# Sparse attention and a four-expert MoE on one core: strided-head loads position by position, a second layer block by block, other numbers in the planner

## The chip, the cores and the metric

One core of a Trainium2 chip runs the whole program. The metric is the device time of one launch in microseconds. One kernel's runs beside another's show differences down to about 1%.

## The reference

Batch 4, 8 heads, 576 positions, 64 values a head, all in float32. Heads 0 to 3 are local (a position sees the 32 positions up to itself), heads 4 to 7 strided (it sees the earlier positions that are equal to it modulo 32). The result, 2304 tokens of 512, goes through four dense experts, all of them for every token.

```
scores = scale * np.matmul(q, k.transpose(0, 1, 3, 2))
mask_local = (rel >= 0) & (rel < stride)                       # stride 32
mask_strided = (rel >= 0) & (pos[None, :] % stride == pos[:, None] % stride)
scores = np.where(masks[None, :, :, :], scores, -1000000000.0)
scores = scores - np.max(scores, axis=-1, keepdims=True)
attn = np.exp(scores); attn = attn / (np.sum(attn, axis=-1, keepdims=True) + 1e-09)
x = np.matmul(attn, v).transpose(0, 2, 1, 3).reshape(B * S, H * D)
for e in range(E):
    h = np.maximum(x @ w1[e], 0.0)
    out += p[:, e:e + 1] * (h @ w2[e])
```

## The kernel before

**Attention.** Two heads make a pair; the 16 pairs run in the order of channels 0, 2, 1, 3 of each batch, so that local (L) and strided (S) pairs alternate. A pair loads q, k, v (`load_qk`, L312 and L318; `load_v`, L328, L332, L339), TensorE transposes q and k (L380, L385), ScalarE evicts them (L344), TensorE makes the scores (L420), VectorE adds the mask and takes the maximum (L429, L434), VectorE or GpSimd subtracts it (L437), ScalarE does the exponential (L442), VectorE the sums (L446 to L448), VectorE or GpSimd the division (L451), TensorE transposes the weights (L477) and multiplies by v (L507), ScalarE evicts into the token buffers (L543, L553), and VectorE subtracts there for the low part (L546). A pair is done in two groups.

**Strided pairs.** Position 32 i + r with residue r sees only positions of its residue: 32 small problems of 18 positions. A partition holds 12 residues of one position, 3 x 18 = 54 partitions a head, partition 18 u + i with u = 0 to 2 and residue r = 10 u + j. All loads are issued by SyncE, one queue, on which at most eight are outstanding: each waits for the one eight before it. The q, k and v tiles of strided pairs are single.

**MoE.** A unit is one expert and one half of its hidden size, eight in all. `plan_first` takes all eight for the first 512 tokens (96 matmuls of 512 columns a unit: L630 the first layer, L646 the second), between the attention's work and after it. Then two parts of 896 tokens take each unit by a product scheme of seven products (L767). Every operand is split in a high and a low part, and three products are made of them: high x high, high x low, low x high. The second layer adds 12 matmuls a bank: `PASS` goes through the three kinds and, within each, the four hidden blocks f. hs 0 to 3 (ScalarE, L634) are the high parts of the blocks, hs 4 to 7 (VectorE, L637) the low parts; `order` shows them as hs_120 to 123 and hs_124 to 127.

**Order.** The program is laid out once by `Plan.run`: each operation has an engine, a duration in us, its tokens and a priority; a list scheduler places the operations and each engine gets its instructions in order of planned start. On the chip each engine runs its list in that order and waits at its head. While TensorE is planned idle before the first MoE matmul, matmuls on zeros are put in (`idle`, L891).

Of the kernel before, what the change touches and what calls it, by code (L numbers as in the profile page):

```python
# [20 lines left out]
VZ = 4.0  # L21
# [3 lines left out]
class Op:  # L25
    __slots__ = ("eng", "dur", "fn", "nxt", "wait", "ready", "prio", "bank", "start", "end", "moe", "cols", "idx")


class Plan:


    SYNC = 0.12
    TICK = 4096 / 1200
# [10 lines left out]
    def add(self, eng, dur, fn, reads=(), writes=(), prio=0.0, bank=None, moe=False, cols=0):  # L44
# [6 lines left out]
        o.cols = cols  # L51
        o.ready = 0.0
# [21 lines left out]
    def run(self, idle):  # L74
# [6 lines left out]
        credit = 0.0  # L81
# [62 lines left out]
        while left:  # L144
# [64 lines left out]
def attn_moe_kernel(  # L209
# [94 lines left out]
    def load_qk(n, which, g):  # L304
# [3 lines left out]
        if kd == "L":  # L308
            t = t[kd][buf(n)]
# [12 lines left out]
    def load_v(n, g):  # L322
        b, c = order[n]
        a = v[b, 2 * c]
        if c < 2:
            t = vst["L"][buf(n)]
            if g != 1:
                nc.sync.dma_start(  # L328
                    out=t[32:LW, 0, :, :], in_=bass.AP(a.tensor, a.offset, [[D, 64], [S * D, 2], [1, D]]))
            t0, t1 = ((1, 4), (4, LT))[g] if g is not None else (1, LT)  # L330
# [15 lines left out]
    def plan_pair(n):  # L346
# [10 lines left out]
        if kd == "L":  # L357
            for g in (0, 1) if n < 4 else (None,):
                gs = (0, 1) if g is None else (g,)
                z = zg[gs[0]]  # L360
                for which, nm in enumerate(("qst", "kst")):
                    add("SP", 1.65 if g is None else 0.95, lambda which=which, g=g: load_qk(n, which, g), (),
                        [f"{nm}L{bf}{i}" for i in gs], z - 16)
                add("SP", 2.4 if g is None else 1.42, lambda g=g: load_v(n, g), (), [f"vstL{bf}{i}" for i in gs], z - (VZ if n < 4 else 0))
        else:
            add("SP", 1.3, lambda: load_qk(n, 0, None), (), ["qstS00", "qstS01"], zg[0] - 16)
            add("SP", 1.3, lambda: load_qk(n, 1, None), (), ["kstS00", "kstS01"], zg[0] - 16)
            add("SP", 2.6, lambda: load_v(n, None), (), ["vstS00", "vstS01"], zg[0] - (VZ if n < 4 else 0))


        for g in range(2):
            z = zg[g]
            for nm, t, dst in (("q", qstv, qTv), ("k", kstv, kTv)):
                key = ("ps", n, "a", nm, g)

                def tr(key=key, t=t, g=g):
# [563 lines left out]
```

## Time and profile before

| | us |
|---|---|
| median of 3 runs (903.64, 907.44, 909.93) | 907.44 |
| the profiled execution | 903.7 |
| its span, first to last instruction | 901.9 |
| TensorE busy | 872.9 (97%) |
| VectorE, ScalarE, GpSimd busy | 528.1, 346.7, 227.8 |
| chain that ended last: TensorE, DMA, VectorE | 87%, 6%, 3% |

A row of the timeline has its start and length, the engine, the line and the tiles (buffer numbers left out: ps and mo are PSUM banks). A busy TensorE need not be at full rate: the granted clock says at which of its two levels (1.2 or 2.4 GHz, 0.5 or 1.0) it ran.

### The profile page before, as it was taken

What the parts mean: (1) busy time and instruction counts of PE and PEld (TensorE: products, weight loads), DVE (VectorE), ACT (ScalarE), POOL (GpSimd) and SP (SyncE); (2) the same over time, 40 slices, a digit from 0 to 9 for tenths busy, and PEclk for the clock granted to TensorE, in tenths of its full rate; (3) what the DMA queues carried; (4) which work ended last, traced back from release to release, by engine and by line L of the source; (5) the groups of instructions that cost most, each with busy time, mean ns of one, the idle gap of its engine ahead of it and who ended that gap; (6) DMA issues with size and microseconds to landing.
All of it is one profiled execution on the core that took longest, in us unless ns stands there. A gap on an engine that the chain in (4) does not pass through costs nothing.

```text
span 901.9 us, 13147 instructions
## 1 busy us (share of the span) xinstructions
PE 872.9 (97%) x5240; PEld 743.1 (82%) x5240; DVE 528.1 (59%) x790; ACT 346.7 (38%) x685; POOL 227.8 (25%) x187
## 2 busy tenths in 40 slices
PE   6889899998999999999999999999999999999998
PEld 4667677786888898888988988889889888898897
DVE  2574676759546455745646656586466574564553
ACT  2563454545223242432523524435235243252340
POOL 1241110326224121321312314152133132131200
PEclk8798899998999999999999999999999999999999
DMA  4474544311222201211211112111111121121002
GB/s 104 129 203 137 142 139 143 93 63 50 92 94 99 99 36 47 93 47 48 88 38 63 47 47 94 47 60 63 36 65 48 47 94 47 47 85 43 15 1 81
DMA packets 65117, 67.95 MB, mean 75 GB/s; under 512 B 36512, under 2 KB 38624, under 8 KB 65056
## 3 DMA queue, kind: packets, MB, share of 16 engines
q1 hardware_dynamic: 65056, 67.12, 23.7%
q8 instruction: 41, 0.67, 0.3%
q14 instruction: 20, 0.16, 0.1%
HBM read 62.39 MB, written 4.72 MB: 74 GB/s over the span
## 4 chain that ended last, share of the span: by engine, by line
PE 87%; DMA 6%; DVE 3%; SPq 2%; ACT 1%; issue 1%; POOL 0%; ACTq 0%; POOLq 0%; DVEq 0%
PE mo L646 26%; PE ps L646 17%; PE ps L767 15%; PE mo L767 15%; PE mo L630 7%; DMA kstS<-in_k 2%; PE ps L420 2%; PE ps L477 1%; PE ps L507 1%; DMA vstS<-in_v 1%; DMA vstL<-in_v 1%; DMA raw<-in_moe_w 1%; PE ps L385 1%; PE ps L380 1%; SPq L318 1%
## 5 line engine op out<-in xcount | busy, mean ns | idle before, releaser
L574 ACT ACTIVATE w2h<-raw 128x512 fp32r<-128x512 f32 x88 | 51.1, 622 | 264.1 <-PE mo L646 144.1
L646 PE MATMUL mo<-w2h,h 128*128 128x512 f32 (+1 forms) x456 | 121.2, 387 | 0.0
L646 PE MATMUL ps<-w2h,h 128*128 128x512 f32 (+1 forms) x448 | 119.0, 387 | 0.0
L655 DVE SCALAR_TENSOR_TENSOR acc<-mo,pr,acc 128x512 f32<-128x512 f32 (+1 forms) x77 | 57.4, 745 | 101.6 <-PE mo L646 101.4
L646 PEld LDWEIGHTS mo<-w2h,h 128*128 128x128 f32 x456 | 85.2, 188 | 17.1
L646 PEld LDWEIGHTS ps<-w2h,h 128*128 128x128 f32 x448 | 83.8, 188 | 16.9
L575 POOL TENSOR_TENSOR w2l<-raw,w2h 128x512 fp32r<-128x512 f32 x27 | 37.9, 1406 | 210.9 <-ACT w2h L574 210.8
L637 DVE SCALAR_TENSOR_TENSOR h<-c,h 128x448 fp32r<-128x448 f32 x96 | 83.7, 884 | 8.8 <-ACT h L634 5.3
L655 DVE SCALAR_TENSOR_TENSOR acc<-ps,pr,acc 128x512 f32<-128x512 f32 (+1 forms) x50 | 37.2, 744 | 66.1 <-PE ps L646 65.8
L646 PE MATMUL mo<-w2h,hs 128*128 128x512 f32 x256 | 72.7, 415 | 3.3 <-ACT hs L634 3.2
L575 DVE TENSOR_TENSOR w2l<-raw,w2h 128x512 fp32r<-128x512 f32 x61 | 59.0, 979 | 15.8 <-ACT w2h L574 15.8
L634 ACT ACTIVATE h<-c 128x448 fp32r<-128x448 f32 x96 | 54.5, 576 | 27.1 <-DVE c L796 25.5
L646 PEld LDWEIGHTS mo<-w2h,hs 128*128 128x128 f32 x256 | 50.0, 199 | 16.6 <-ACT hs L634 5.7
L646 PE MATMUL mo<-w2l,h 128*128 128x512 f32 (+1 forms) x228 | 60.6, 387 | 0.0
L646 PE MATMUL ps<-w2l,h 128*128 128x512 f32 (+1 forms) x224 | 59.5, 387 | 0.0
L646 PEld LDWEIGHTS mo<-w2l,h 128*128 128x128 f32 x228 | 42.6, 188 | 8.9
L646 PEld LDWEIGHTS ps<-w2l,h 128*128 128x128 f32 x224 | 41.9, 188 | 8.7
L783 ACT ACTIVATE u<-mo 128x448 f32<-128x448 f32 x48 | 26.1, 545 | 46.0 <-PE mo L767 45.7
L796 DVE TENSOR_TENSOR c<-mo,u 128x448 f32<-128x448 f32 x48 | 29.5, 615 | 19.8 <-PE mo L767 19.2
L796 DVE TENSOR_TENSOR c<-ps,u 128x448 f32<-128x448 f32 x48 | 29.5, 615 | 19.7 <-PE ps L767 19.7
L646 PE MATMUL mo<-w2l,hs 128*128 128x512 f32 x128 | 39.4, 421 | 0.0
L783 ACT ACTIVATE u<-ps 128x448 f32<-128x448 f32 x48 | 26.1, 545 | 29.0 <-PE ps L767 28.7
(239 smaller groups left out, 1739.9 us busy)
## 6 DMA issues: line engine op xcount, KB each, us to landing
raw<-in_moe_w SPq DMA_DIRECT2D x44, 1024.0 KB
out<-acc SPq DMA_DIRECT2D x17, 256.0 KB
qstS<-in_q SPq DMA_DIRECT2D x16, 162.0 KB
kstS<-in_k SPq DMA_DIRECT2D x16, 162.0 KB
vstS<-in_v SPq DMA_DIRECT2D x32, 81.0 KB
vstL<-in_v SPq DMA_DIRECT2D x12, 192.0 KB
qstL<-in_q SPq DMA_DIRECT2D x12, 144.0 KB
kstL<-in_k SPq DMA_DIRECT2D x12, 144.0 KB
```

Source lines behind the costliest of these rows:

```text
L318: nc.sync.dma_start(out=t[:, h].rearrange("p t d -> p (t d)"), in_=bass.AP(a.tensor, a.offset + h * S * D, [[10 * D, 3], [32 * D, 18], [1, ...
L420: nc.tensor.matmul(s[a, o:o + W], lhsT, rhs, start=True, stop=True)
L574: add("ACT", 0.62, lambda: nc.scalar.activation(out=hi(), in_=src(), func=AF.Copy), [tok], [name + "h"], z)
L575: add("VP", VP, lambda e: engine(e).tensor_tensor(out=lo(), in0=src(), in1=hi().bitcast(F32), op=ALU.subtract), [tok, name + "h"], [name + ...
L630: nc.tensor.matmul(pt[:, 0:TA], w[:, c % 2, (f % 2) * P:(f % 2) * P + P], (xl if i == 1 else xh)[c], start=j == 0, stop=j == 11)
L634: nc.scalar.activation(out=dst(), in_=src(), func=AF.Relu)
L637: nc.vector.scalar_tensor_tensor(out=dst(), in0=src(), scalar=0.0, in1=hi().bitcast(F32), op0=ALU.max, op1=ALU.subtract)
L646: nc.tensor.matmul(pt, ht[f][:, ts], wt[f][:, cs], start=j == 0, stop=j == 11)
L655: nc.vector.scalar_tensor_tensor(out=a, in0=pt, scalar=sc, in1=a, op0=ALU.mult, op1=ALU.add)
L767: nc.tensor.matmul(pt, wq[a][i == 2][:, j, f * P:f * P + P], xq[b][i == 1][j], start=bool(first) and n == 0, stop=True, skip_group_check=True)
L783: add("ACT", 0.55, lambda: nc.scalar.activation(out=late["u"][i], in_=held[key][:, 0:TH], func=AF.Copy), [key, "late2"], [f"u{i}"], zz)
L796: add("DVE", 0.6, lambda: nc.vector.tensor_tensor(out=late["c"][c], in0=held[key][:, 0:TH], in1=late["u"][i], op=ALU.add), [key, f"u{i}"], ...
```

## The change

1. `load_qk` and `load_v` for strided pairs: the source's outer dimension is 18 (positions), then 3, then the contiguous residues. Partition 3 i + u takes the place of 18 u + i; the mask, and the source and target patterns of the evictions (`xsrc`, `cols`), follow.
2. The first four pairs' local loads are no longer issued in two parts (`g` goes away).
3. The second layer's 12 matmuls go hidden block by hidden block, three kinds for each.
4. The planner: other durations (only two lines shown), 0.18 us after a TensorE operation before another engine may use it, and loads that follow each other on one modelled wire.

```diff
+    DRAIN = 0.18
+    LAND = 1.9
             if e == "SP":
-                o.end += 2.1
+                wire = max(wire, o.end) + o.xfer
+                o.end = wire + self.LAND
...
-                x.ready = max(x.ready, o.end + (self.SYNC if x.eng != e else 0.0))
+                x.ready = max(x.ready, o.end + (self.SYNC + self.DRAIN * (e == "PE") if x.eng != e else 0.0))
...
-            ts = slice(0, 6) if g is None else slice(3 * g, 3 * g + 3)
             for h in range(2):
                 nc.sync.dma_start(
-                    out=t[:, ts, h, :], in_=src[b, 2 * c + h].rearrange("(t p) d -> p t d", p=LW)[:, ts])
+                    out=t[kd][buf(n)][:, :, h, :], in_=src[b, 2 * c + h].rearrange("(t p) d -> p t d", p=LW))
...
                     out=t[:, h].rearrange("p t d -> p (t d)"),
-                    in_=bass.AP(a.tensor, a.offset + h * S * D, [[10 * D, 3], [32 * D, 18], [1, 12 * D]]))
+                    in_=bass.AP(a.tensor, a.offset + h * S * D, [[32 * D, 18], [10 * D, 3], [1, 12 * D]]))
...
-                        in_=bass.AP(a.tensor, a.offset + (h * S + 6 * par) * D, [[10 * D, 3], [32 * D, 18], [1, 6 * D]]))
+                        in_=bass.AP(a.tensor, a.offset + (h * S + 6 * par) * D, [[32 * D, 18], [10 * D, 3], [1, 6 * D]]))
...
-                add("ACT", (0.3, 0.33)[c > 1], ev, [key], [f"{nm}T{kd}{bf}{g}"], z + 0.2)
+                add("ACT", (0.41, 0.44)[c > 1], ev, [key], [f"{nm}T{kd}{bf}{g}"], z + 0.2)
...
-            dd = nel / 960 + 0.07
+            dd = nel / 960 + 0.15
...
-                        return bass.AP(a.tensor, a.offset, [list(a.ap[0]), [1, 6], [10, 3], [32, i1 - i0]])
+                        return bass.AP(a.tensor, a.offset, [list(a.ap[0]), [1, 6], [32, i1 - i0], [10, 3]])
...
-        passes = list(enumerate(PASS))
+        passes = list(enumerate((i, f) for f in range(NKF) for i in range(3)))
...
-    strided = (p // 18 == c // 18) & (c % 18 <= p % 18) | (p >= 54)
+    strided = (p % 3 == c % 3) & (c // 3 <= p // 3) | (p >= 54)
```

SyncE, the first loads after those of pair 0's first half and the masks. Before (qstL_131 is pair 0, qstS pairs 1 and 3, qstL_132 pair 2):

```order
L312 DMA qstL_131<-in_q 96x3x64 x2
L312 DMA kstL_134<-in_k 96x3x64 x2
L318 DMA qstS<-in_q 54x1x768 x2
L318 DMA kstS<-in_k 54x1x768 x2
L312 DMA qstL_132<-in_q 96x3x64 x2
L312 DMA kstL_135<-in_k 96x3x64 x2
L328 DMA vstL_137<-in_v 64x2x64
L332 DMA vstL_137<-in_v 96x3x64 x2
L312 DMA qstL_132<-in_q 96x3x64 x2
L312 DMA kstL_135<-in_k 96x3x64 x2
L332 DMA vstL_137<-in_v 96x5x64 x2
L318 DMA qstS<-in_q 54x1x768 x2
```

Of the change, from the same point (the masks) on:

```order
L321 DMA qstS<-in_q 54x1x768 x2
L321 DMA kstS<-in_k 54x1x768 x2
L315 DMA qstL_132<-in_q 96x6x64 x2
L315 DMA kstL_135<-in_k 96x6x64 x2
L330 DMA vstL_137<-in_v 64x2x64
L333 DMA vstL_137<-in_v 96x8x64 x2
L340 DMA vstS<-in_v 54x1x384 x4
L321 DMA qstS<-in_q 54x1x768 x2
L321 DMA kstS<-in_k 54x1x768 x2
```

The first strided pair's q and k move ahead by four issues, its v (vstS) stands ahead of the next strided pair's q and k instead of behind them.

TensorE, from the last matmuls of the first unit's first layer to its second layer. Before:

```order
L630 MATMUL mo<-xh_115,a22l 128x512
L385 MATMUL ps<-ident,qstS 128x54 x6
L385 MATMUL ps<-ident,kstS 128x54 x6
L385 MATMUL ps<-ident,qstS 128x54 x6
L385 MATMUL ps<-ident,kstS 128x54 x6
L646 MATMUL mo<-w2h_84,hs_120 128x512
L646 MATMUL mo<-w2h_85,hs_121 128x512
L646 MATMUL mo<-w2h_86,hs_122 128x512
L646 MATMUL mo<-w2h_87,hs_123 128x512
L646 MATMUL mo<-w2l_88,hs_120 128x512
```

Of the change:

```order
L627 MATMUL mo<-xh_115,a22l 128x512
L417 MATMUL ps<-kTL_145,qTL_142 64x96 x10
L643 MATMUL mo<-w2h_84,hs_120 128x512
L643 MATMUL mo<-w2l_88,hs_120 128x512
L643 MATMUL mo<-w2h_84,hs_124 128x512
L643 MATMUL mo<-w2h_85,hs_121 128x512
L643 MATMUL mo<-w2l_89,hs_121 128x512
L643 MATMUL mo<-w2h_85,hs_125 128x512
L474 MATMUL ps<-ident,pmL 96x128 x4
L643 MATMUL mo<-w2h_86,hs_122 128x512
```

The strided transposes have gone from between the two layers (one stands ahead of the first layer's last twelve matmuls, three behind the second layer's first twelve), local scores stand there, and a low part (hs_124) is the third matmul's operand, where it was the ninth's.

## Rows read from the trace of the kernel before

**Rows 1.** Busy time by stage: five stretches of the span, with the busy time and instruction count of PE, PEld, DVE, ACT and POOL, then the granted clock, the DMA share and GB/s. The cuts are the first matmul of the first MoE layer (46.20), the end of the third MoE unit, in which the attention ends (204.30), the end of the next second layer (232.57) and the first matmul of the product scheme (320.90).

```profile
0.00:46.20 46.20, 36.25 (x404) 27.01 (x405) 19.04 (x47) 18.46 (x43) 10.61 (x21) 0.78 0.46 121
46.20:204.30 158.10, 145.52 (x1660) 119.09 (x1657) 102.72 (x206) 79.00 (x182) 33.65 (x33) 0.95 0.46 129
204.30:232.57 28.27, 25.08 (x97) 19.91 (x96) 22.00 (x26) 11.81 (x24) 13.89 (x9) 0.88 0.23 75
232.57:320.90 88.33, 88.24 (x386) 71.79 (x385) 48.45 (x54) 26.36 (x48) 24.02 (x17) 1.00 0.26 93
320.90:902.00 581.10, 577.81 (x2701) 505.30 (x2699) 335.88 (x459) 211.06 (x392) 145.66 (x108) 1.00 0.16 54
```

**Rows 2.** The chain of work that ended last, in order of time, 0 to 130 us: start, length, what. Three of its DMA pieces.

```profile
8.16 9.75 DMA kstS<-in_k
...
27.16 11.95 DMA vstS<-in_v
...
59.20 11.61 DMA kstS<-in_k
```

**Rows 3.** Single microseconds with the DMA share and GB/s in the last two columns: 165 and 167 (the loads of strided pairs, issued from 157.60 to 164.8, are in flight and nothing else), 194 (one weight load).

```profile
165.00:166.00 1.00, 1.00 (x20) 0.70 (x19) 0.79 (x2) 1.00 (x3) 1.00 (x2) 1.00 0.18 74
...
167.00:168.00 1.00, 1.00 (x19) 0.85 (x16) 1.00 (x1) 1.00 (x4) 0.82 (x1) 1.00 0.20 80
...
194.00:195.00 1.00, 1.00 (x6) 0.81 (x5) 0.97 (x2) 0.00 (x0) 0.83 (x2) 1.00 0.92 354
```

**Rows 4.** SyncE's queue in order of time: start, length, line, tile, number of DMAs.

```profile
0.74 0.90 SPq L312 DMA_DIRECT2D qstL<-in_q  x2
...
5.68 1.69 SPq L318 DMA_DIRECT2D qstS<-in_q  x2
...
7.41 1.45 SPq L318 DMA_DIRECT2D kstS<-in_k  x2
...
24.82 3.04 SPq L339 DMA_DIRECT2D vstS<-in_v  x4
```

**Rows 5.** TensorE in order of time up to the first MoE matmul: start, length, line, tile, count, and in brackets the idle time before and what ended it.

```profile
3.73 0.69 PE L380 MATMUL ps<-ident,qstL 96*128 96x96 f32 x3
...
9.06 1.04 PE L420 MATMUL ps<-kTL,qTL 64*64 64x96 f32 x20
...
18.04 0.86 PE L385 MATMUL ps<-ident,kstS 54*128 54x54 f32 x6 [0.66 <-DMA kstS<-in_k]
...
31.82 0.55 PE L385 MATMUL ps<-ident,kstS 54*128 54x54 f32 x6 [1.54 <-DVE pmL L437]
...
34.12 0.82 PE L385 MATMUL ps<-ident,kstS 54*128 54x54 f32 x6 [0.94 <-DMA kstS<-in_k]
...
39.16 1.52 PE L507 MATMUL ps<-pTS,vstS 54*64 54x54 f32 x22 [0.26 <-DMA vstS<-in_v]
...
46.20 0.50 PE L630 MATMUL mo<-xh,a11h 128*128 128x512 f32 x1
```

**Rows 6.** Two stretches with the columns of the first group; the granted clock is the third column from the end.

```profile
34.40:44.30 9.90, 9.64 (x106) 7.54 (x104) 3.70 (x9) 4.08 (x10) 0.99 (x1) 0.50 0.71 173
68.50:74.50 6.00, 5.08 (x25) 4.25 (x26) 1.41 (x4) 1.32 (x3) 0.99 (x1) 0.50 0.59 144
```

**Rows 7.** TensorE in order of time, 68 to 74 us.

```profile
68.73 0.88 PE L385 MATMUL ps<-ident,kstS 54*128 54x54 f32 x6 [3.56 <-DMA kstS<-in_k]
...
70.94 0.85 PE L385 MATMUL ps<-ident,kstS 54*128 54x54 f32 x6 [0.69 <-DMA kstS<-in_k]
...
71.73 2.08 PE L646 MATMUL mo<-w2h,hs 128*128 128x512 f32 x4
```

**Rows 8.** TensorE's waits between 46.2 and 204.3 us: who waited for whom, us in total, times, the longest.

```profile
PE ps L477 <- DVE pmS L451: 2.0, 1, 2.0
...
PE ps L477 <- POOL pmL L451: 1.9, 3, 0.8
...
PE ps L477 <- DVE pmL L451: 1.3, 2, 1.0
...
PE ps L420 <- ACT kTL L344: 1.2, 2, 1.0
...
PE ps L507 <- ACT pTL L344: 0.8, 2, 0.5
...
PE ps L507 <- DMA vstL<-in_v: 0.3, 1, 0.3
```

**Rows 9.** TensorE, then VectorE, in order of time around 219 us, in the fourth unit (the first one after the attention).

```profile
219.50 0.80 PE L646 MATMUL mo<-w2h,hs 128*128 128x512 f32 x1 [2.96 <-ACT hs L634]
...
218.76 0.68 DVE L637 SCALAR_TENSOR_TENSOR hs<-mo,hs 128x512 fp32r<-128x512 f32 x1
...
221.72 0.68 DVE L637 SCALAR_TENSOR_TENSOR hs<-mo,hs 128x512 fp32r<-128x512 f32 x1
```

**Rows 10.** TensorE at the start of the second layer of the fifth unit; and one piece of the chain in order of time from the product scheme, twelve matmuls of 512 columns with nothing in their way.

```profile
243.45 1.35 PE L646 MATMUL mo<-w2h,hs 128*128 128x512 f32 x4
...
340.83 2.72 PE ps L646 x12
```

**Rows 11.** ScalarE's groups by shape, 0 to 240 us: total busy us, mean ns of one, idle before. A PSUM eviction of 324 columns into consecutive columns, and one of as many into columns 32 apart.

```profile
L344 ACT ACTIVATE kTS<-ps 128x324 f32<-128x324 f32 x16 | 7.0, 438 | 13.5 <-PE ps L385 13.4
...
L553 ACT ACTIVATE xr<-ps 128x324 f32<-128x324 f32 x8 | 6.0, 750 | 3.4 <-PE ps L507 3.3
```

More of the change, by code (lines that the diff above doesn't have):

```diff
@@ L25 @@
 class Op:
-    __slots__ = ("eng", "dur", "fn", "nxt", "wait", "ready", "prio", "bank", "start", "end", "moe", "cols", "idx")
+    __slots__ = ("eng", "dur", "fn", "nxt", "wait", "ready", "prio", "bank", "start", "end", "moe", "cols", "idx", "xfer")
 class Plan:
     SYNC = 0.12
+    DRAIN = 0.18
+    LAND = 1.9
     TICK = 4096 / 1200
@@ L42, in __init__, with add @@
         self.mix = mix
-    def add(self, eng, dur, fn, reads=(), writes=(), prio=0.0, bank=None, moe=False, cols=0):
+    def add(self, eng, dur, fn, reads=(), writes=(), prio=0.0, bank=None, moe=False, cols=0, xfer=0.0):
         o = Op()
@@ L51, in add @@
         o.cols = cols
+        o.xfer = xfer
         o.ready = 0.0
@@ L80, in run @@
         allocs = {t: [] for t in self.banks}
-        credit = 0.0
+        credit = wire = 0.0
         began = False
@@ L302, in buf, with load_qk @@
         return n // 2 % 2 if order[n][1] < 2 else 0
-    def load_qk(n, which, g):
+    def load_qk(n, which):
         b, c = order[n]
@@ L326, in load_v @@
             t = vst["L"][buf(n)]
[L327 to L330, printed above, removed]
+            nc.sync.dma_start(
+                out=t[32:LW, 0, :, :], in_=bass.AP(a.tensor, a.offset, [[D, 64], [S * D, 2], [1, D]]))
             for h in range(2):
                 nc.sync.dma_start(
-                    out=t[:, t0:t1, h, :],
-                    in_=bass.AP(a.tensor, a.offset + h * S * D + (64 * t0 - 32) * D, [[D, LW], [64 * D, t1 - t0], [1, D]]))
+                    out=t[:, 1:LT, h, :],
+                    in_=bass.AP(a.tensor, a.offset + h * S * D + 32 * D, [[D, LW], [64 * D, LT - 1], [1, D]]))
         else:
@@ L357, in plan_pair @@
         if kd == "L":
[L358 to L364, printed above, removed]
-        else:
-            add("SP", 1.3, lambda: load_qk(n, 0, None), (), ["qstS00", "qstS01"], zg[0] - 16)
-            add("SP", 1.3, lambda: load_qk(n, 1, None), (), ["kstS00", "kstS01"], zg[0] - 16)
-            add("SP", 2.6, lambda: load_v(n, None), (), ["vstS00", "vstS01"], zg[0] - (VZ if n < 4 else 0))
+            for which, nm in enumerate(("qst", "kst")):
+                add("SP", 0.95, lambda which=which: load_qk(n, which), (), [f"{nm}L{bf}{i}" for i in (0, 1)],
+                    zg[0] - 16, xfer=1.3)
+            add("SP", 1.6, lambda: load_v(n), (), [f"vstL{bf}{i}" for i in (0, 1)], zg[0] - (VZ if n < 4 else 0), xfer=2.2)
+        else:
+            for which, nm in enumerate(("qst", "kst")):
+                add("SP", 1.45, lambda which=which: load_qk(n, which), (), [f"{nm}S0{i}" for i in (0, 1)],
+                    zg[0] - 16, xfer=1.5)
+            add("SP", 2.9, lambda: load_v(n), (), ["vstS00", "vstS01"], zg[0] - (VZ if n < 4 else 0), xfer=1.5)
         for g in range(2):
@@ L455, in plan_pair @@
             tok, tm, ts = f"pm{kd}{gi}", f"mx{par}{gi}", f"sm{par}{gi}"
-            dd = nel / 960 + 0.07
-            vp = (dd, nel * 2.0e-3 + 0.05)
+            dd = nel / 960 + 0.15
+            vp = (dd, nel * 1.6e-3 + 0.2)
             need = [f"{x}T{kd}{bf}{i}" for x in "qk" for i in ((gi,) if kd == "S" else range(gi + 1))]
-            add("PE", ng * (0.212, 0.16)[c > 1], qk, need, [key, tok], z + 3, key, cols=2 * nel)
+            add("PE", 0.2 + ng * (0.166, 0.116)[c > 1], qk, need, [key, tok], z + 3, key, cols=2 * nel)
             add("DVE", dd, mask, [key, "mask" + kd], [tok], z + 3.2)
-            add("DVE", dd + 0.1, rmax, [tok], [tm], z + 3.4)
+            add("DVE", dd, rmax, [tok], [tm], z + 3.4)
             add("VP", vp, bsub, [tm], [tok], z + 3.6)
-            add("ACT", nel / 1200 + 0.11, ex, (), [tok], z + 3.8)
+            add("ACT", nel / 1200 + 0.2, ex, (), [tok], z + 3.8)
             add("DVE", dd + 0.45, rsum, [tok], [ts], z + 4)
@@ L547, in xlo @@
                                 out=cols(xl[c]), in0=src(), in1=cols(xh[c].bitcast(F32)), op=ALU.subtract)
-                        add("ACT", 0.25, xhi, [key], [f"xh{c}{g}"], z + 7.2)
-                        add("DVE", 0.3, xlo, [key, f"xh{c}{g}"], [f"xl{c}{g}"], z + 7.4)
+                        add("ACT", 0.42, xhi, [key], [f"xh{c}{g}"], z + 7.2)
+                        add("DVE", 0.44, xlo, [key, f"xh{c}{g}"], [f"xl{c}{g}"], z + 7.4)
                     else:
@@ L584, in plan_load @@
     def plan_load(which, u, z):
-        add("SP", 3.0, lambda: load_w(which, u), (), [f"raw{which}"], z)
+        add("SP", 0.4, lambda: load_w(which, u), (), [f"raw{which}"], z, xfer=3.2)
     def plan_w2(z):
```

21 lines of the change are left out of this document (9 added, 12 removed).

## The prediction

> **What bounds the kernel now.** I read the stages first [rows 1]. From 320.9 us on TensorE is busy 577.8 of 581.1 us at the full clock (the rest is the end: last sums and output): nothing of the change makes its matmuls fewer, so those 581 us stay. From 232.57 to 320.90 it is as full. What can move lies ahead of that: TensorE idles 10 of the first 46.2 us at a mean granted clock of 0.78, and 12.6 of the next 158.1 us at 0.95.
>
> The chain says who made it wait [rows 2]: three pieces are loads of strided pairs, 9.75, 11.95 and 11.61 us from issue to landing. The DMA view says why they take so long [rows 3]. With only such loads in flight the DMA share is 0.18 to 0.20, three of sixteen engines, and they move 74 to 80 GB/s; a weight load in flight has a share of 0.92 and 354 GB/s. Both are about 24 to 25 GB/s an engine. So a strided load uses three engines, as many as its outer dimension counts. One head of q is 162 KB, 54 KB an engine, 2.25 us at 24 GB/s; and the second head's transposes stand 2.30 and 2.21 us behind the first's [rows 5, 7], that pace. A strided pair's q, k and v (972 KB) hold those three engines for 13.5 us. Local and weight loads have their share on the same engines and wait behind.
>
> In the timeline TensorE waits until 18.04 for the first strided k, and around 31.82, 34.12 and 39.16 for the next strided loads [rows 5] (31.82 is put down to VectorE, but it stands one load's pace ahead of 34.12; I take it for the load). From 34.4 to 44.3 it then runs at 1.2 GHz [rows 6]. At 68.73 it waits for k once more and is again at 1.2 GHz [rows 6, 7].
>
> **The load, part 1 of the change.** The outer dimension becomes 18. Over sixteen engines at most, the busiest gets two of the 18 rows, whether nine engines take two each or sixteen share unevenly: 18 KB, 0.75 us instead of 2.25. A pair's loads then hold the queue 4.5 us, not 13.5. The bounds are three engines, as now, and the weight load's 354 GB/s (0.46 us). I take 0.75, since both counts follow the row's own rule (three rows, three engines).
> The Trainium skill, "DMA: Bandwidth & Descriptors", section "Why a DMA increments its semaphore by 16 and not by 1", says that a load uses the largest number of engines up to 16 that divides the outer sizes of both its sides. With 3 and 54 that is 3, and the trace agrees (0.18 of 16); with 18 and 54 it would be 9, which no run here shows yet. By it a head takes 0.75 us; by a reading of "18" as all sixteen engines it would be 0.46, and the sum would gain about 0.3 us more at each load waited for.
>
> **The start.** The first strided q stood behind ten issues and stands behind six; a pair of issues takes 0.90 [rows 4], so it starts 1.9 us earlier and the last k issue begins at 6.2 instead of 8.16. Pair 0's q, two issues of 0.45 from 0.74 on, is used at 3.73 [rows 4, 5], 2.5 us after the last of them began. 6.2 + 2.5 + 0.75 is 9.5. Pair 0's scores end at 10.1 [rows 5], so the loads are no longer what is late: four transposes of about 0.5 us follow, to 12.2 instead of 18.9. Lead: 6.7. Part 2 (local loads whole) delays pair 0's first transposes by some tenths, since its q lands later, but pair 0's last scores not; I cost it at nothing behind those.
> The waits at 31.82, 34.12 and 39.16, 2.7 us in sum, go: v is now issued ahead of the next q and k, as the order of SyncE shows, and all three land in a third of the time. The 9.64 us of work at 1.2 GHz would take 4.8 less at 2.4; I count half, 2.4, since the new order has its own gaps. Against it 0.9 us: of pair 2 the second group's transposes and products now stand behind the start of the first MoE layer, less some transposes of pair 4 that stand ahead of it (twenty score matmuls took 1.04, [rows 5], the scale that I use). So 6.7 + 2.7 + 2.4 - 0.9 = 10.9, and the first MoE matmul at about 34.4. Bounds: the lead alone, 5.8; and VectorE, which has 19.0 us of work ahead of that point [rows 1] and can't begin before the first scores at 9.06: 28.1, so 17.2. I stay between, at the rows' own waits.
>
> **The stall at 68 us.** 3.56 + 0.69 idle, and 5.08 us of work at half the clock [rows 6, 7], 2.5 lost: 6.8. That stall also hid the evictions between the two layers. Without it the second layer begins 1 us behind the first (the twenty local scores), and its third and sixth matmuls want low parts from VectorE, 0.68 us each [rows 9]; I put 0.8 for that. Gain 6.0; bounds 2.0 and 6.8. The local v's 0.3 [rows 8] goes too, since it waited behind strided loads.
>
> **Small waits.** The other five kinds between 46.2 and 204.3 sum to 7.2 us [rows 8], and the clock after them costs some 3 more (0.95 over 158.1 us is 15.8 at 1.2 GHz, less the 6 at 68 us, half of it lost, part of it idle anyway). They are ends of the softmax chain: TensorE's list has the transposes too early. The planner's numbers move toward the rows: an eviction from 0.30 or 0.33 to 0.41 or 0.44 (measured 0.438, [rows 11]), each VectorE step 0.08 longer, 0.18 after TensorE; about 0.5 us a chain, ten waits, some of them shorter: I take 4, with bounds of 0 and 10. A new order also makes new waits; the largest of this kind was 2.0, and three such, 6 us, are the bound on that side.
>
> **The second layer block by block.** In the steady units the first four matmuls take 1.35 us instead of a third of 2.72 [rows 10], 0.91, since the fourth wants the last block's high part, which is ready only then. A unit takes 22.08 (88.33 by four, [rows 1]) against 96 x 0.2267 = 21.76. Now that part is the tenth matmul's, two microseconds later: 0.3 x 4 = 1.2. In the fourth unit, right after the attention, TensorE waits 2.96 for a high part [rows 9]. But the low parts of the last two blocks come at 219.44 and 222.40 there, and the new order wants them ninth and twelfth within the same bank, as the old one wanted them eleventh and twelfth. The bank can't end before 222.4 in either. I cost this unit at nothing (bounds: 6.5 gained, its 28.27 against 21.76; 3 lost).
>
> **Evictions.** Writing 324 columns 32 apart takes 750 ns, consecutive ones 438 [rows 11]. The new pattern is 3 columns 10 apart, then steps of 32: between 438 and, as an upper bound, twice 750. Sixteen of them, 12 us at most, lie beside ScalarE's 79 busy of 158 us; uncovered, the last pair's two cost 1.5. I take 750, no change. Fewer local issues (part 2) only relieve SyncE.
>
> **Sum.** 10.9 + 6.0 + 0.3 + 4 + 1.2 = 22.4 us, from the profiled execution's 903.7 (span 901.9 and 1.8 around it): **881.3**. The median of the runs shown is 907.44, 0.4% above that execution, so a median may lie some 3 us higher.
>
> **Rivals.**
> *Softmax holds the start* (0.15): loads land early, but the chain of VectorE, ScalarE and GpSimd sets the pace, as VectorE's 19 us suggest. Start 5.8, stall 6.0, 0.3 and 1.2, no small wait gained, some 2 lost: 903.7 - 11.3, 892.
> *More than I take* (0.12): the start at its bound 17.2 and 8 of the small waits: 871. For it speaks that all but the fourth unit's stall would then be gone; against it, that every engine would have to be on time.
> *The loads stay slow* (0.06): still three engines. Then the earlier issue gives 1.9, v ahead of the next q and k costs those 4.5, the stall at 68 us stays, 1.2 and 2 come from the rest: 903. The share of exactly three speaks against it.
> *Slower: low parts waited for* (0.05). The third matmul of each bank wants VectorE's work. If in every unit the first bank ended as late as the fourth unit's (7.2 us behind the first layer's end, instead of 2.72, 4.5 more), seven other units cost 31: 903.7 - 22.4 + 31 is 912. It decides from 3.2 us a unit. Against it: VectorE is that full (22.0 of 28.3) only there; before, it is busy 103 of 158 us, after, 48 of 88 [rows 1].
>
> **How the numbers follow.** My case (872 to 890) has 0.62. The range 868 to 896 holds it, most of "softmax" and half of "more": about 0.8. A measurement of this kernel can tell about 1% from no change, so faster means below 894.7: 0.62 + 0.12 + 0.11 of "softmax" is 0.85. Same: the rest of that, slow loads and a mild case of low parts, 0.10. Slower 0.05.
>
> **What would show it.** A strided load alone in flight has a DMA share near 0.56 (nine of sixteen); the first strided transposes end near 12 and the first MoE matmul stands near 34; TensorE no longer waits for q or k of a strided pair; the steady units take 21.8. I am wrong if the share stays near 0.19, if the first MoE matmul stands behind 41, if TensorE waits for hs in several units, or if the part from the product scheme on takes other than 581.

## The result and the profile after

The changed kernel takes **879.75 us** (median of 4 runs, 876.83 to 881.53) against 905.54 for the kernel before (median of 4); the ratio is 0.971, 95% interval 0.966 to 0.976. The profiled execution took 876.83 us with a span of 875.0, so it is 26.9 us shorter in span than the profiled one of before; forecast were 22.4 us and 881.3, and the time lies in the likeliest case's own range, 872 to 890.

The stages of the kernel after, with the columns of [rows 1] and cut at the same places of the program: first MoE matmul, end of the third unit, end of the fourth unit, first product.

```profile
0.00:33.77 33.77, 30.34 (x391) 22.75 (x394) 18.94 (x47) 17.66 (x42) 9.81 (x20) 0.90 0.73 195
33.77:178.55 144.78, 142.15 (x1678) 114.59 (x1677) 102.25 (x204) 79.40 (x182) 38.04 (x37) 0.99 0.48 134
178.55:206.92 28.37, 24.72 (x97) 19.42 (x96) 22.71 (x27) 13.06 (x26) 13.88 (x10) 0.88 0.24 75
206.92:293.95 87.03, 87.03 (x385) 72.07 (x384) 43.49 (x52) 25.88 (x46) 26.36 (x18) 1.00 0.28 94
293.95:875.00 581.05, 577.82 (x2701) 505.29 (x2699) 324.29 (x457) 215.69 (x392) 154.81 (x110) 1.00 0.16 54
```

The start gives 12.4 us, the first three units 13.3, the later four 1.3, the product part nothing. The fourth unit gives nothing either, and it has changed its wait. TensorE in order of time, two transposes of the first strided pair and the first MoE matmul:

```profile
10.80 0.55 PE L382 MATMUL ps<-ident,kstS 54*128 54x54 f32 x6 [1.29 <-DMA kstS<-in_k]
...
11.77 0.54 PE L382 MATMUL ps<-ident,kstS 54*128 54x54 f32 x6
...
33.77 0.48 PE L627 MATMUL mo<-xh,a11h 128*128 128x512 f32 x1
```

The strided transposes end at 12.3 where they ended at 18.9 [rows 5]; one wait for a strided k, 1.29 us, is left ahead of them. A microsecond in which only loads of strided pairs are in flight has this DMA share and GB/s (last two columns), where it had 0.18 to 0.20 and 74 to 80 [rows 3]:

```profile
102.00:103.00 1.00, 0.91 (x7) 0.50 (x5) 0.28 (x2) 0.60 (x1) 0.00 (x0) 1.00 0.57 178
```

That is nine of sixteen engines. TensorE's waits in the first three units (33.77 to 178.5 us), the answer to [rows 7, 8]:

```profile
PE ps L474 <- POOL pmS L448: 1.5, 1, 1.5
PE mo L643 <- DVE hs L634: 0.4, 1, 0.4
PE mo L627 <- DVE xl L543: 0.2, 1, 0.2
```

The wait of 3.56 us for k, the wait for a local v and all but one wait for the softmax are gone. In the fourth unit (the answer to [rows 9]) TensorE, then VectorE, then GpSimd, in order of time:

```profile
193.76 1.22 PE L643 MATMUL mo<-w2h,hs 128*128 128x512 f32 x2 [2.34 <-DVE hs L634]
...
196.72 1.22 PE L643 MATMUL mo<-w2h,hs 128*128 128x512 f32 x2 [1.31 <-DVE hs L634]
```

```profile
189.31 0.68 DVE L634 SCALAR_TENSOR_TENSOR hs<-mo,hs 128x512 fp32r<-128x512 f32 x1
189.91 1.12 DVE L576 TENSOR_TENSOR tmp<-xr 128x448 f32<-128x448 f32 x1
190.96 0.68 DVE L572 TENSOR_TENSOR a12l<-raw,a12h 128x512 fp32r<-128x512 f32 x1
191.56 1.55 DVE L741 TENSOR_TENSOR t3l<-tmp,t3h 128x448 fp32r<-128x448 f32 x1
193.03 0.68 DVE L634 SCALAR_TENSOR_TENSOR hs<-mo,hs 128x512 fp32r<-128x512 f32 x1
193.63 0.95 DVE L741 TENSOR_TENSOR b22l<-xr,b22h 128x448 fp32r<-128x448 f32 x1
194.50 1.56 DVE L741 TENSOR_TENSOR t2l<-tmp,t2h 128x448 fp32r<-128x448 f32 x1
195.98 0.68 DVE L634 SCALAR_TENSOR_TENSOR hs<-mo,hs 128x512 fp32r<-128x512 f32 x1
```

```profile
191.18 1.45 POOL L576 TENSOR_TENSOR tmp<-xr,tmp 128x448 f32<-128x448 f32 x1 [0.62 <-DVE tmp L576]
192.59 1.51 POOL L741 TENSOR_TENSOR t1l<-tmp,t1h 128x448 fp32r<-128x448 f32 x1
194.18 1.40 POOL L576 TENSOR_TENSOR tmp<-xr,tmp 128x448 f32<-128x448 f32 x1
```

TensorE waits for the low parts that VectorE makes at 193.03 and 195.98. Ahead of each of them VectorE has work that is not needed yet: sums and low parts (tmp, t, b22l) for the product part, some 100 us later, and a low part of the next unit's weights (a12l). Between the first and the last low part of this unit (186.14, not shown, to 195.98) stand eight such instructions. The unit is 6.6 us longer than a later one (28.36 against 21.76): 3.65 us are these two waits, and some 2.5 the granted clock, which is 0.50 behind the first of them while TensorE has 5.09 us of work (row in the last section).

### The profile page after: what moved, and what is told of

Same layout as the page of the kernel before. It is cut to its first block, busy times and chain, and to the rows that moved or that the text cites. A ratio compares the mean times of both kernels' runs of the same rounds, so it can differ in the third digit from the quotient of the medians.

```text
span 875.0 us, 13183 instructions
## 1 busy us (share of the span) xinstructions
PE 862.1 (99%) x5245; PEld 734.1 (84%) x5248; DVE 511.7 (58%) x785; ACT 351.7 (40%) x685; POOL 242.9 (28%) x192
## 4 chain that ended last, share of the span: by engine, by line
PE 92%; DMA 2%; DVE 2%; SPq 1%; ACT 1%; issue 1%; DVEq 0%; ACTq 0%
PE mo L643 27%; PE ps L643 17%; PE ps L764 16%; PE mo L764 16%; PE mo L627 8%; PE ps L417 2%; PE ps L504 2%; PE ps L474 1%; PE ps L382 1%; DMA qstL<-in_q 1%; PE ps L379 1%; DMA raw<-in_moe_w 1%; DMA kstS<-in_k 1%; SPq L315 1%; SPq L321 0%
## 5 line engine op out<-in xcount | busy, mean ns | idle before, releaser
L571 ACT ACTIVATE w2h<-raw 128x512 fp32r<-128x512 f32 x88 | 54.4, 630 | 241.4 <-PE mo L643 138.9
L643 PE MATMUL mo<-w2h,h 128*128 128x512 f32 (+1 forms) x456 | 148.7, 387 | 0.0
L643 PE MATMUL ps<-w2h,h 128*128 128x512 f32 (+1 forms) x448 | 146.1, 387 | 0.0
L572 POOL TENSOR_TENSOR w2l<-raw,w2h 128x512 fp32r<-128x512 f32 x44 | 67.8, 1545 | 200.0 <-ACT w2h L571 196.0
L643 PE MATMUL mo<-w2h,hs 128*128 128x512 f32 x256 | 87.8, 408 | 4.2 <-DVE hs L634 4.1
L643 PE MATMUL mo<-w2l,h 128*128 128x512 f32 (+1 forms) x228 | 88.3, 387 | 0.0
L643 PE MATMUL ps<-w2l,h 128*128 128x512 f32 (+1 forms) x224 | 86.8, 387 | 0.0
L643 PE MATMUL mo<-w2l,hs 128*128 128x512 f32 x128 | 50.7, 396 | 0.0
L572 POOL TENSOR_TENSOR s2l<-tmp,s2h 128x512 fp32r<-128x512 f32 x14 | 18.1, 1296 | 105.1 <-PE mo L764 52.3
L793 DVE TENSOR_TENSOR c<-ps,u 128x448 f32<-128x448 f32 x48 | 29.5, 614 | 23.8 <-PE ps L764 16.5
L572 DVE TENSOR_TENSOR w2l<-raw,w2h 128x512 fp32r<-128x512 f32 x44 | 35.3, 803 | 12.6 <-ACT w2h L571 12.6
L793 DVE TENSOR_TENSOR c<-mo,u 128x448 f32<-128x448 f32 x48 | 29.5, 615 | 21.1 <-PE mo L764 20.5
```

Source lines behind the costliest of these rows:

```text
L571: add("ACT", 0.62, lambda: nc.scalar.activation(out=hi(), in_=src(), func=AF.Copy), [tok], [name + "h"], z)
L572: add("VP", VP, lambda e: engine(e).tensor_tensor(out=lo(), in0=src(), in1=hi().bitcast(F32), op=ALU.subtract), [tok, name + "h"], [name + ...
L643: nc.tensor.matmul(pt, ht[f][:, ts], wt[f][:, cs], start=j == 0, stop=j == 11)
L793: add("DVE", 0.6, lambda: nc.vector.tensor_tensor(out=late["c"][c], in0=held[key][:, 0:TH], in1=late["u"][i], op=ALU.add), [key, f"u{i}"], ...
```

## The experiments

All spans and stages in the table are from profiled executions; a stage ends at the first matmul of the next one. "Three units" are the first three, in which the attention's work is mixed in, "each later" is one of units five to eight. The ratio is that of the runs to those of the kernel before on the same chip, with its 95% interval. Each stage is read from one execution, and runs of one kernel differ by up to 7.8 us (e3), so a difference of one or two us between two stages stands only where a wait in the trace goes with it.

| kernel | median us | ratio | span | start | three units | fourth | each later |
|---|---|---|---|---|---|---|---|
| before | 904.29 to 906.05 | 1 | 901.9 | 46.20 | 158.11 | 28.26 | 22.08 |
| after | 879.75 | 0.971 (0.966 to 0.976) | 875.0 | 33.77 | 144.79 | 28.36 | 21.76 |
| e1 layout alone | 886.07 | 0.978 (0.973 to 0.982) | 883.4 | 33.52 | 152.21 | 28.31 | 22.08 |
| e2 layout undone | 893.94 | 0.987 (0.982 to 0.992) | 892.2 | 45.60 | 149.40 | 29.12 | 21.76 |
| e3 old numbers | 867.73 | 0.959 (0.954 to 0.964) | 865.7 | 32.47 | 142.43 | 22.73 | 21.76 |
| e4 old second-layer order | 880.22 | 0.971 (0.967 to 0.976) | 878.1 | 32.58 | 147.54 | 28.43 | 22.08 |
| g1 layout, block order | 880.05 | 0.974 (0.971 to 0.978) | 877.7 | 34.24 | 152.63 | 22.73 | 21.76 |
| g2 layout, whole loads | 880.56 | 0.974 (0.972 to 0.976) | 877.3 | 32.44 | 147.12 | 28.35 | 22.08 |
| g3 old attention numbers | 877.31 | 0.971 (0.969 to 0.973) | 871.4 | 32.26 | 142.90 | 28.14 | 21.76 |
| e6 higher VectorE price | 871.58 | 0.964 (0.963 to 0.965) | 870.5 | 33.58 | 146.93 | 21.78 | 21.76 |
| e5 block order alone | 900.33 | 0.994 (0.993 to 0.996) | 900.0 | 47.71 | 161.52 | 22.75 | 21.76 |
| e8 split loads | 880.18 | 0.972 (0.969 to 0.975) | 878.5 | 32.23 | 148.76 | 29.45 | 21.76 |
| h1 as e3, higher price | 870.47 | 0.962 (0.960 to 0.964) | 868.3 | 33.24 | 144.46 | 22.43 | 21.76 |
| h2 as g3, higher price | 868.98 | 0.961 (0.959 to 0.963) | 866.0 | 32.51 | 142.89 | 22.43 | 21.76 |

**Layout alone (e1)**: the kernel before with the source pattern, the eviction patterns and the mask of the change.

```diff
-                    in_=bass.AP(a.tensor, a.offset + h * S * D, [[10 * D, 3], [32 * D, 18], [1, 12 * D]]))
+                    in_=bass.AP(a.tensor, a.offset + h * S * D, [[32 * D, 18], [10 * D, 3], [1, 12 * D]]))
...
```

> The kernel before with the strided loads laid out position by position and nothing else (its instructions stand in the order of before). Theory (the strided loads were what was late): the last strided k is issued at 8.2 us as before, but lands in a third of the time, so the strided transposes end near 14 instead of 18.9; the waits at 31.8, 34.1 and 39.2 go; the first MoE matmul stands at 37 to 40, the stall at 68 us (about 6.5) goes, the small waits stay: 889 us, 884 to 895. Rival (the planner's numbers and the new order are what gave the time): the first MoE matmul stays behind 43 and the time is 897 or more.

The theory holds and was too cautious about the start: the strided transposes end at 13.2, and the first MoE matmul stands at 33.5, not at 37 to 40. Its stages, with the columns of [rows 1]:

```profile
0.00:33.50 33.50, 29.93 (x401) 23.04 (x404) 18.51 (x46) 17.45 (x41) 9.65 (x20) 0.90 0.58 160
33.50:185.70 152.20, 142.40 (x1660) 116.49 (x1657) 102.92 (x207) 79.39 (x183) 34.80 (x34) 0.97 0.48 136
185.70:214.00 28.30, 25.11 (x97) 20.02 (x96) 22.01 (x26) 11.79 (x24) 13.87 (x9) 0.88 0.23 75
214.00:302.30 88.30, 88.21 (x385) 71.77 (x385) 48.43 (x54) 26.39 (x48) 24.04 (x17) 1.00 0.27 93
```

With every instruction in the order of before, the start is 12.7 us shorter and the first three units 5.9; from the fourth unit on nothing differs from [rows 1] by more than 0.1. The layout alone is worth 18.5 us of span. TensorE's waits in the first three units still sum to 9.7, all but 0.4 for the attention's chain, and these have grown: beside the waits for strided k and local v the idle time was 8.0 before, and is 9.8 here.

**Layout undone (e2)**: the same lines the other way round in the changed kernel.

```diff
-                    in_=bass.AP(a.tensor, a.offset + h * S * D, [[32 * D, 18], [10 * D, 3], [1, 12 * D]]))
+                    in_=bass.AP(a.tensor, a.offset + h * S * D, [[10 * D, 3], [32 * D, 18], [1, 12 * D]]))
...
```

> The changed kernel with the old layout of the strided loads, three outer rows, everything else as changed. Theory: the DMA share of a strided load is 0.18 to 0.20 again, its pair holds the queue 13.5 us, v now stands ahead of the next q and k: the start is back at 41 to 46, the stall near 68 us is back or stands elsewhere at the same size: 899 to 908 us. Rival (numbers and order gave the time): 890 or less.

The time lies between the two. The start is back, and so are the three engines, as the last two columns of a microsecond show in which strided loads are in flight:

```profile
102.00:103.00 1.00, 1.00 (x20) 0.93 (x15) 0.97 (x3) 1.00 (x4) 0.66 (x1) 1.00 0.21 80
```

The stall near 68 us stands elsewhere, as the theory allowed. TensorE waits for a low part, since ScalarE, ahead of the high parts in its list, waits for the next unit's weights, which SyncE issued at 61.09, behind the strided loads, and at 45.62 in the kernel after (ScalarE, then TensorE):

```profile
68.23 0.63 ACT L571 ACTIVATE a11h<-raw 128x512 fp32r<-128x512 f32 x1 [7.19 <-DMA raw<-in_moe_w]
...
71.92 0.79 PE L643 MATMUL mo<-w2h,hs 128*128 128x512 f32 x1 [6.58 <-DVE hs L634]
```

Even so the first three units stay 8.7 us shorter than before: the waits of the attention's chain there are 1.3 us instead of 8.0, so the rest of the change is worth more than the theory had given it. Undoing the layout costs 17.2 us of span, near the 18.5 that it gave alone.

**Old numbers (e3)**: the changed kernel with the planner's durations, landing times and hand-over times of before.

```diff
-            dd = nel / 960 + 0.15
-            vp = (dd, nel * 1.6e-3 + 0.2)
+            dd = nel / 960 + 0.07
+            vp = (dd, nel * 2.0e-3 + 0.05)
...
-                x.ready = max(x.ready, o.end + (self.SYNC + self.DRAIN * (e == "PE") if x.eng != e else 0.0))
+                x.ready = max(x.ready, o.end + (self.SYNC if x.eng != e else 0.0))
```

> The changed kernel with the planner's durations of before (new layout, whole local loads and the second layer block by block stay). Theory: only the small waits of the softmax chains come back, 4 us by the forecast: 881 to 888 us, the first MoE matmul within 3 us of 33.8. Rival (the measured durations are the main cause): 893 or more, first MoE matmul behind 40.

Both missed: it is faster than the change by 9.3 us in span and 12 in the medians, and with h2 below the fastest kernel here. Its stages up to the end of the fourth unit, then VectorE and GpSimd there:

```profile
0.00:32.40 32.40, 29.69 (x384) 22.05 (x387) 18.32 (x45) 17.58 (x42) 10.94 (x21) 0.89 0.68 189
32.40:174.85 142.45, 139.85 (x1682) 114.92 (x1679) 104.01 (x209) 83.62 (x190) 42.85 (x40) 0.99 0.50 140
174.85:197.60 22.75, 22.09 (x97) 17.96 (x97) 17.47 (x21) 9.51 (x18) 11.05 (x9) 1.00 0.30 94
```

```profile
184.49 0.69 DVE L629 SCALAR_TENSOR_TENSOR hs<-mo,hs 128x512 fp32r<-128x512 f32 x1
185.09 1.03 DVE L567 TENSOR_TENSOR a11l<-raw,a11h 128x512 fp32r<-128x512 f32 x1
186.05 1.71 DVE L736 TENSOR_TENSOR t4l<-tmp,t4h 128x448 fp32r<-128x448 f32 x1
187.68 1.28 DVE L629 SCALAR_TENSOR_TENSOR hs<-mo,hs 128x512 fp32r<-128x512 f32 x2
```

```profile
185.57 1.71 POOL L567 TENSOR_TENSOR a12l<-raw,a12h 128x512 fp32r<-128x512 f32 x1
```

The old numbers' plan puts four instructions among the low parts instead of eight, the last two low parts stand together, the granted clock stays at 1.00, and the unit takes 22.73 us: 5.6 of the 9.3. The start gives 1.3, the first three units 2.4. Of the theory only the place of the first MoE matmul held (32.5).

**Old second-layer order (e4)**: the changed kernel with `PASS` again.

```diff
-        passes = list(enumerate((i, f) for f in range(NKF) for i in range(3)))
+        passes = list(enumerate(PASS))
```

> The changed kernel with the second layer's old order (all high parts by high weights, then by low weights, then the low parts). Theory: the four units ahead of the product part take 22.08 each instead of 21.76, 1.3 us in sum, and the fourth unit's wait moves from the low parts (2.3 and 1.3 us) to a high part of ScalarE's with 28.3 us for the unit as before: 880 to 883 us. Rival (the new order is worth more, since low parts also come late in the first three units' softmax work): 885 or more.

As the theory has it: 22.08 us a later unit, 28.43 for the fourth with a wait of 3.0 for ScalarE's high part. In the changed kernel's plan the block order gives no more than its 1.3 us; what it adds in the fourth unit it loses there by the low parts. The start shrinks by 1.2; the first three units grow by 2.8, with a wait of 5.6 us at 56.8 for a division on GpSimd, whose chain stands on ScalarE behind the second unit's weights (4.3 us of waiting for them).

**Layout and block order (g1); layout and whole local loads (g2)**: the layout of e1 with the line of e4 the other way round, and with part 2 of the change (old numbers in both).

```diff
-                out=t[:, ts, h, :], in_=src[b, 2 * c + h].rearrange("(t p) d -> p t d", p=LW)[:, ts])
+                out=t[kd][buf(n)][:, :, h, :], in_=src[b, 2 * c + h].rearrange("(t p) d -> p t d", p=LW))
...
```

> The kernel before with two edits: the new layout of the strided loads and the second layer block by block; local loads in two parts and the planner's numbers stay as before. Theory (the block order is worth 1.3 us in the four units ahead of the product part and 5.6 us in the fourth unit, wherever the plan puts at most four other instructions between that unit's first and last low parts on VectorE, as it does here; whole local loads are worth some 10 us in the first two units): fourth unit 22.7 us, the first two units as with the layout alone (55.7 and 59.6), 877 to 880 us. Rival (the block order is worth only the 1.3 us of the forecast): fourth unit 28.3, 884 us or more. Second rival (whole loads are worth nothing): 866 to 870 us.

> The kernel before with the new layout and the local loads whole; the second layer's old order and the planner's old numbers stay. Theory: the first two units take 50 to 52 and 53 to 55 us (as with the old numbers and the block order), the fourth unit 28.3 with a wait for a high part, since the plan puts eight other instructions among its low parts, the later four 22.08 each: 873 to 877 us. Rival (whole loads are worth nothing, as the forecast had it): 884 us or more.

In g1 the fourth unit is the 22.73 us of the theory and the time is at its upper end; the first three units, 152.63 in sum, are as with the layout alone (152.21), though the second is 3.5 us longer and the third 3.9 shorter. In g2 the first unit (51.1 us) is as expected, the second (59.1) is not, and the time misses the interval by 3.6. Whole loads are worth 6.1 us of span beside the layout alone, but 12.0 beside layout and block order (g1 to e3). The ratios show the second clearly (0.974 to 0.959, intervals apart); those of the first (0.978 and 0.974) have intervals that overlap.

**Old attention numbers (g3)**: the changed kernel with the attention's durations of before, the loads' prices and the 0.18 us kept.

```diff
-            add("ACT", nel / 1200 + 0.2, ex, (), [tok], z + 3.8)
+            add("ACT", nel / 1200 + 0.11, ex, (), [tok], z + 3.8)
...
```

> The changed kernel with the old durations of the attention's instructions alone (transposes, evictions, scores, softmax steps, x parts); the loads' new prices and the 0.18 us behind TensorE stay. The plan still puts eight others among the fourth unit's low parts. Theory (the attention's new durations cost the start and the first unit some 3.4 us, the fourth unit's order the rest of the 9 to 12 us by which the old numbers were faster): start 32 to 33, first unit 50.5 to 52, fourth unit 28.3: 875 to 878 us. Rival (the loads' prices or the 0.18 cost it): start and first unit as in the changed kernel, 33.8 and 52.7, 879 to 882 us.

As the theory has it in the profiled execution: 3.4 us come back in start and first three units (1.5 and 1.9), none in the fourth. It is the fastest of g3's runs, though; in the medians the gain is 2.4 us, and the ratio to the kernel before is 0.971 for both kernels, so the runs together don't show it. What such a loss is made of can be seen in the last group of the second strided pair. VectorE, GpSimd and TensorE of the changed kernel, then of g3:

```profile
39.27 1.01 DVE L836 TENSOR_SCALAR psums<-psums 128x18 f32<-128x18 f32 x1
...
40.76 0.48 DVE L443 TENSOR_REDUCE sm<-pmS 128x6 f32<-128x324 f32 x1
...
41.75 1.08 POOL L448 TENSOR_TENSOR pmS<-pmS,sm 128x324 f32<-128x324 f32 x1 [1.51 <-DVE sm L445]
...
42.88 0.60 PE L474 MATMUL ps<-ident,pmS 128*128 128x128 f32 x3 [1.46 <-POOL pmS L448]
```

```profile
36.81 0.48 DVE L443 TENSOR_REDUCE sm<-pmS 128x6 f32<-128x324 f32 x1
...
38.44 0.73 POOL L448 TENSOR_TENSOR pmS<-pmS,sm 128x324 f32<-128x324 f32 x1 [0.40 <-DVE sm L445]
...
39.88 1.01 DVE L836 TENSOR_SCALAR psums<-psums 128x18 f32<-128x18 f32 x1
...
41.72 0.49 PE L474 MATMUL ps<-ident,pmS 128*128 128x128 f32 x3
```

GpSimd divides in both. The new numbers put VectorE's work on the experts' weights p (psums) ahead of this group's sum, which so begins at 40.76, and TensorE waits 1.46 us for the division; in g3 the sum stands ahead of that work, and TensorE has no wait for it.

**A higher price for VectorE (e6)**: the changed kernel, one line.

```diff
-    VP = (0.69, 1.38)
+    VP = (1.2, 1.5)
```

> The changed kernel with one number more nearer the trace: the price of a split, a sum or a difference on VectorE 1.2 us instead of 0.69 (they take 0.61 alone and about 1.55 beside GpSimd) and 1.5 instead of 1.38 on GpSimd. The plan then puts four others, not eight, among the fourth unit's low parts. Theory (these others are what made TensorE wait 2.3 and 1.3 us and run at half the clock after it): the fourth unit takes 22 to 24 us instead of 28.4, the time is 872 to 876 us. Rival (low parts are late by the work ahead of them, wherever the others stand): fourth unit 27 or more, 878 us or more.

As the theory has it, and a little better than its intervals: 21.78 us for the fourth unit, no wait in it and the full clock, and 871.58 us. The third unit grew by 2.8 (to 41.1) with hardly a wait in it: the plan puts 490 TensorE instructions there instead of 439, which the first unit has fewer of. The first unit is no shorter for that, since TensorE waits in it for a low part, behind ScalarE's wait of 5.4 us for the second unit's weights:

```profile
56.82 0.79 PE L643 MATMUL mo<-w2h,hs 128*128 128x512 f32 x1 [3.80 <-DVE hs L634]
```

**Block order alone (e5); split loads (e8)**: the line of e4 the other way round in the kernel before; the local loads of the first four pairs in two parts again in the changed kernel. The second edit also gives the planner other issue prices for local v loads (1.42 and, where whole, 2.4 instead of 1.6), so it undoes part 2 not quite alone.

```diff
-            for which, nm in enumerate(("qst", "kst")):
+            for g in (0, 1) if n < 4 else (None,):
...
```

> The kernel before with the second layer block by block and nothing else. Its plan puts four others, not eight, among the fourth unit's low parts on VectorE. Theory (that is what the block order needs to pay there): fourth unit 22.7 us instead of 28.3, the later four 21.76 each instead of 22.08, start 46.2 as before, the first three units within 1 us of 158.1: 896 to 900 us. The forecast's own term (1.2 us, nothing in the fourth unit): 901 to 904 us.

> The changed kernel with the first two local pairs' loads in two parts again, all else as changed. Theory (whole loads are worth some 6 us whatever the numbers, as between the layout alone and the layout with whole loads): start 34 to 35, the first three units 148 to 150 us in sum instead of 144.8, fourth unit 28.3: 884 to 888 us. Rival (they were worth that only in the old numbers' order): 878 to 882 us.

In e5 the fourth unit (22.75) and the later ones are as expected, 6.8 us; the start and the first three units grow by 4.9, since the plan's order there changes too and the strided loads are still late (six waits for k, 12.0 us in sum); the time, 900.33, lies just above the theory's interval and below the other. In e8 the first three units take 148.76, as the theory says, with a wait of 4.7 us for a low part, again behind ScalarE's wait for the second unit's weights (5.9 us); the start is 1.5 us shorter against it, where the theory had it longer. The time is in the rival's interval. In span split loads cost 3.5 us, in the medians 0.4: with the new numbers, whole loads are worth little or nothing that can be measured.

**Both kinds of gain together (h1, h2)**: `VP = (1.2, 1.5)` in e3 and in g3.

```diff
-    VP = (0.69, 1.38)
+    VP = (1.2, 1.5)
```

> New layout, whole local loads and the block order with the planner's old numbers (867.7 us), and the price of splits, sums and differences raised to 1.2 us on VectorE and 1.5 on GpSimd. Theory (the price helps only among the low parts): fourth unit 21.8 to 22.7, the rest within 1 us: 864 to 868 us. Rival (the raised price moves low parts of the third unit late, as it did in the changed kernel, where that unit grew by 2.8 us): 868 to 872 us.

> The changed kernel with the attention's old durations (start and first three units 3.4 us shorter) and the raised price of splits, sums and differences (fourth unit 6.6 us shorter, third 2.8 longer). Theory (the two add up, since one acts on the attention and the other on what stands among the low parts): 866 to 870 us. Rival (each reorders the whole plan, so nothing adds up): outside 863 to 873 us.

h2's time is as the theory says, its parts are not quite: the fourth unit gains 5.9 of the 6.6 us, and the first three lose nothing. h1 fits its rival's interval and its reason in part: the third unit grows by 1.5 us, the second by as much, the first shrinks by 1.0; the three lose 2.0 us together, with 3.5 us of waits for the softmax and none for a low part. Neither can be told from e3 by its runs (865.13 to 872.90).

## Why the prediction was right, and where only its sum was

**Layout: right.** Forecast were 17.2 us (start 10.9, stall 6.0, a local v 0.3), and e1 gives 18.5. Nine engines, the end of the transposes at 12.2, the first MoE matmul at 34.4: nine, 12.3 and 33.77 measured. Within the start the terms were off and cancel. The loads were still what is late there: k lets its transposes begin at 10.80 after a wait of 1.29, not at 9.5, and pair 0's scores end at 9.0, not 10.1, so 12.2 was met by luck. The "1.9 us earlier" of the issue was not needed: e1 has the old issue order and reaches the MoE at 33.52. And e1, which runs the same instructions as the kernel before, has 6.4 us less idle time up to there, where 9.4 were forecast, and 6.3 us less busy time, where 2.4 were forecast for the clock: before, the granted clock was at its lower level from 13.7 to 23.9 and from 34.2 to 44.4, in e1 only from 12.3 to 19.1. The stall of 6.0 and 0.3 is 5.9 in e1, a net figure: the waits for k and local v (4.6) and 3.1 us of busy time go, other waits grow by 1.8.

**Evictions: right.** 324 columns in the new pattern take 764 ns, 750 before [rows 11]:

```profile
L550 ACT ACTIVATE xr<-ps 128x324 f32<-128x324 f32 x8 | 6.1, 764 | 3.2 <-PE ps L504 3.1
```

**Block order in the later units: right**, 1.2 forecast, 1.3 measured (88.32 to 87.04).

**Small waits.** Of their 7.2 us (the trace has a sixth kind of 0.6, so 7.8) a single wait of 1.5 is left in the kernel after. The forecast gave this gain to the planner's numbers; e3, with the old numbers, has it too.

**Whole local loads at nothing: wrong.** They are worth 12.0 us of span beside layout and block order, and 6.1 beside the layout alone, which is hardly clear of the noise. A wait for their transfer does not show: in the first three units none for a local q or k stood in [rows 8] or stands in e1. The plan orders the rest otherwise, and TensorE's idle time in the first three units goes from 10.6 us in g1 to 2.6 in e3. Which of the moved instructions does it was not tried.

**"The planner's numbers move toward the rows", 4 us gained: wrong in sign.** Layout and block order being there, the other two parts make a table of four spans: split loads with old numbers 877.7 (g1), with new 878.5 (e8); whole loads with old numbers 865.7 (e3), with new 875.0 (after). With split loads the new numbers do what the forecast said: 3.9 us in the first three units, 2.0 in the start. But whole loads with the old numbers give more in the same places (10.2 and 1.8), and the two don't add: after whole loads the new numbers cost 2.4 and 1.3 there. And in either row they cost the fourth unit 5.6 to 6.7 us. The step that failed is that truer durations make a better plan. In the fourth unit the price that mattered was not among the changed ones: with 1.2 instead of 0.69 us for VectorE's share of that work, and 1.5 instead of 1.38 for GpSimd's (e6), it is 6.6 us shorter. In the first unit the loads' new prices have a mark of their own: SyncE issues the second unit's weights at 45.62 in the kernel after, at 34.53 in e3, and in every kernel with these prices ScalarE waits for them (1.0 us after, 7.2 in e2, 4.3 in e4, 5.9 in e8, 2.5 in g3, 5.4 in e6, 2.4 in h2), in none with the old ones. No run changes the loads' prices alone, so what they cost in the kernel after is not shown.

**The fourth unit at nothing: right for this plan, and by chance.** The reason given ("the bank can't end before 222.4 in either") took VectorE's order as fixed. With eight other instructions among the low parts the unit takes 28.1 to 29.5 us in either order of the second layer; with the block order and four (g1, e3, e5, e6) or five (h1, h2) it takes 21.8 to 22.8, that is 5.5 to 6.6 less; 6.5 was the bound that the forecast named and didn't take. The rival "low parts waited for" is what stands here, 3.65 us of waits, in this one unit and not in every one (0.4 us in the first three).

So the layout was right as a mechanism, and the rest of the sum was near since errors cancel: 8.4 us beyond the layout's 18.5 where 5.2 were forecast for numbers and block order, out of about +17.7 for whole loads and block order together and -9.3 for the numbers.

## What to carry to other kernels

Count the outer rows of a load's pattern in the DMA share before anything else; an outer dimension of 3 left thirteen engines idle, and putting 18 outermost gave 18.5 us with no instruction moved. Numbers in a planner are not judged one by one against the trace: each reorders the whole list, so measure the plan with and without them. A consumer that takes its operands in a new order gained here only where little else was queued among their producers: look at the list of the engine that makes them. And where an engine waits at the head of its list for a load, as ScalarE did here for weights, look for the wait of another engine behind it: the profile names only the last link.

## What the runs showed of the hardware

A VectorE instruction with two SBUF inputs that comes up while GpSimd is in one of its own ends about 0.48 us after that ends, and its record is so much longer: of the same shape, 0.61 us alone and 1.55 beside GpSimd. At 191.56 `t3l` takes 1.55 us and ends at 193.11; GpSimd's `tmp` ends at 192.63. At 194.50 `t2l` ends at 196.06, GpSimd's at 195.58. In e3 `t4l` ends at 187.76, GpSimd's at 187.28. `a12l`, which begins at 190.96, ahead of GpSimd's `tmp` at 191.18, takes 0.68. Low parts hs, with one input in PSUM, take 0.68 beside GpSimd (189.31) or not. The Trainium skill, "SBUF — State Buffer", section "Who interferes with whom", says that a VectorE instruction with two SBUF inputs contends with a GpSimd instruction that reads SBUF, that the shared port pair is an exclusive lock, and that an instruction with at most one SBUF input, outside the 2-port modes, does not contend; these rows agree.

With the wait of 2.34 us in the fourth unit the granted clock fell to the lower level, though TensorE had been busy 131.1 of the 133 us before at 1.00 (the granted clock is the third column from the end):

```profile
60.00:193.00 133.00, 131.14 (x1542) 107.01 (x1540) 99.42 (x188) 75.18 (x169) 38.41 (x35) 1.00 0.40 113
...
193.80:200.20 6.40, 5.09 (x11) 3.60 (x12) 5.26 (x7) 1.53 (x3) 1.70 (x2) 0.50 0.17 33
```

A strided load of 162 KB takes SyncE about 0.80 us to issue (1.60 for two, at 79.08 in the kernel after), a pace of some 200 GB/s; the 178 GB/s above are near it. Whether more than nine engines would bring anything was not tried.
